# A planned order from one table of wanted times, in place of ranks, rounds and shifts

## The chip, the core and the metric

The kernel runs on one core of a Trainium2 chip. That core has TensorE (PE, with its weight loads as PEld), VectorE (DVE), ScalarE (ACT), GpSimd (POOL), and SyncE (SP), which here issues the transfers between HBM and the on-chip memories. The metric is the device time of one execution in microseconds. Three executions of the kernel before gave a median of 616.97 us (616.25 to 618.5). A difference of about 0.5% of that, some 3.1 us, is the smallest that a measurement of this kernel tells from no change.

## What is computed

The reference is one attention layer followed by one feed-forward layer, in float32:

```python
k_sum = k.reshape(B, H, nb, block, D).max(axis=3)
v_sum = v.reshape(B, H, nb, block, D).mean(axis=3)
scores_l = where(|i - j| < 16, scale * q @ k.T, -1e9)
scores_s = scale * q @ k_sum.T + log(block)
a = softmax(concat([scores_l, scores_s]))
attn = a @ concat([v, v_sum])
xn = (x - mean(x)) / sqrt(var(x) + 1e-6) * g_ln     # x = attn, heads side by side
out = x + relu(xn @ w_ch1) @ w_ch2
```

There are 4 batches, 8 heads, 768 positions, a head size of 64, blocks of 32 positions, a model width of 512 and a hidden width of 2048. So the attention is narrow (each row sees some 31 neighbours and 24 block summaries), and nearly all multiplications are those of the feed-forward layer.

## The kernel before

**Tiles.** The 3072 rows of x are 24 tiles of 128 rows. The first six tiles (batch 0, "early") are done with float32 products; the other eighteen ("late") with each operand split into two float16 halves. The names that the profile shows: `spare_x` holds the early keys, queries and values; `s` is a tile of scores; `p` the probabilities, `pp` their transposes, `o` the product with the values, `v` (on PE) the block means of the early values, `x` a finished tile of the attention, `xt` its normalised transpose. `raw` is a weight matrix as fetched, `m` the same with its bits merged by three DVE instructions (`merge_w`), `gram` small products that give its scale, `low` products that give the low half of a weight. `h` is the first product of the feed-forward layer (`g1`, L1005) and `a` the second (`g2`, L1028). A group of g1 takes two tiles of x, so there are twelve groups of eight steps.

**Order.** No engine's program is written in the order of the Python loops. `Plan` (L157 to L424) records every operation with its engine, its inputs and outputs; a list scheduler then decides the order, and `issue` (L402 to L424) emits the operations sorted by the start that the scheduler gave them. On each engine the chip runs them in just this order, so every record of the profile stands at one line, L425 of the profile's count. All of the transfers go through SP's one queue.

**The scheduler.** `schedule` (L341) walks through all 2808 operations. For each engine it keeps the operations that could start and takes the one with the lowest `rank`. It charges an operation its `busy` time from `cost` (L289); for a transfer it charges three numbers from the table `MOVE` (L175): the time on SP, the time that the transfer holds the queue, and the tail until its data may be read. It also holds TensorE's two clock levels, a cost for a change of kind on TensorE, and the port that DVE and POOL share. It runs forward or, with `back`, from the end to the start.

**Ranks before.** `issue` first gives each operation a rank by the longest way to the end, adds one number per stage from the table `ORDER`, runs `schedule` forward and backward up to three times (`ROUNDS`), keeps the best, adds one number per stage and engine from the table `SHIFT`, and runs forward once more. A stage is one call of a function that `@pl.step` marks, for example `early_qk(3)`.

The steps at the start that the prediction speaks of are these. `warm` (L1076) gives PE 36 transposes that need only `ident`. `gain` needs one small transfer, a PE product and some DVE instructions. `fetch_k0` brings the early keys in four transfers, `batch_k(0, hp)` reduces each on DVE to `kmax`, `early_k` (L800) puts the key tile together with copies on ACT and POOL, and `early_qk` (L810) is the product on PE. `fetch_v0` and `batch_v0` (L585, L592) bring six value tiles and a last piece, and add their block means in one chain of matmuls on PE. `clear` and `late_masks` are POOL's memsets and copies.

Of the kernel before, what the change touches and what calls it, by code (L numbers as in the profile page):

```python
# [24 lines left out]
B, H, S, D = 4, 8, 768, 64  # L25
# [18 lines left out]
ROUNDS = 3  # L44
# [11 lines left out]
    "c-k$Ne_YS^7RQfmchNQq`4MVX5)<o^a?>>{gl-`+tEP0f-7A}W$2FQq=K497MpWyngjs%cjYab-yRo#cmW^qqCE=<@`^81#b)P-"  # L56
    "De|#UG`h4E+_c`bFdY#vKXV*wcPnm7)V0L-"
    "4<dz|gIVxS+Cmkq|b{v$_&PmbFn$371<s6Z&d>}oP6wmkc15)u@W=+m!ryR`kk4uYcr3I{YoMqNI$!s<I@BK>}>S{J6*evy*(n0oSl=A+R6h>T"
    "^&Ss@gn}zev_c62ERnpFnCD%C4Zk8@^Zl`}pdpAgP*nj#8`?g5I?@0~;W)a=Yj;2b<Ig;@#x+@Lh%$GZwO(f?@=~DY|rKs<uz%gc3d!?_wmST5"
    "E$H;fuNOEP*iE62wnulDL#{b6bBfi}w##!<#`%p?fEnP2>dLEM||IKW7CiQxl?df86g0no&OaA2Cl{Jlh%%;9+Hjtd-"  # L60
    "Mw#{gRZ6LlvU-}02Djnl7sUUAe9Ue+nSDlnD~P|2wOJ>nL*#RY9M6?Yd5@S?4>Swrd3QKCk>AH|X70VsMzn{UpQQ))rRRAzuO-iEoC$uJJEf^N"
    "rD2DqDep@g{w+NjZZ>8QypmT2yyg*W*&Alv&PatHNeiDt3tOdH_Kiay1!Yp{CvZ*8yC8neHYtX8Q@}Bf8dChtZr*`&;@_dh>3<+LnwafqmOH@g"
    "L*9>yF<TO1=0wi*Xe=5|mY|~*5$t`^Yzw*=4fn+tSbI%sJuhdGSqzvY<x3INzVJ&a5v+YS!G))p%R1^oS6=8RA3hz)X-"
    "gBe@0M=B#SHY3g)U+~mo}lNkXup^Jbg?2fz-DKOuT=RuA&!*KcW@%8}PE(X0%fCgjxJXwD?;y=V#Duq**jN%YpwGwAX&M^cFpmPwbliN=v=X8b"
    "_P82gAX{^8({yu&IEr&Ob<RyokQ3FN>O1p|$N`eC;)}$9TVFzFEJnW{E@DKiKS<$I+}2e}P%p5Om|q9^xMZ!w}ZIfOZD7V*$0i&EMJe(sttYU1"
    "(NAkF_J;Pr*JBF5}3h?^*EpOnTPKYyyAxp+--"
    "%JDiwZs3CEJ*|KPKMID#G^)UKv2{hXuW;Pd0+<Sn@N@?a4vu_C7LOu!9dlG%TOJ2_r@5S+Ej`T`AdmHeN0q7(j?4scDI(_gH`aVO?A1Ia@&}$h"
    "QcR~BLW6kbgrB~2W&)=bCxClYJS?*?Oc+w<#-3JWLqQ779fxnacIzRfCc-`ST0{*KirB<IQ{*ivhcf!!zB`|-"
    "VXEfTrL4WxYs{~z)B$u)1=aE)i(be2X%`(vJ&v?!e>aEMBhxi^qzKxye|0pn~XWZfPYy<r9bVCQe<d%evX5a}<DR?6K@`8`jUS_e>9t_ql=w~O"
    "mJ&m6GliPzjsRQ^HvS)--8>YSSnkW~ul2(mv$3M_W5ghKu>&C*z=9y-TIj{Mm6b^R<=*|HwLdpG=-"  # L70
    "<u7Fi>Q8R6kg`h%l>F{7MMG6hAVyOk6uQDMJ_peqLuHSH=EV!+w|e%=;k6Z9wpWh-uGnRsz1Ro-qqCIY#JWF9&Kc@zi9=&OTTt+q-"
    "W^KfIp+NJbdxGv>KoHK|dS7`=wZB31^;0kMDu&LF#etZ*~RT%Zc;)A@U=Bf4prnG5&(DucWRQ*3kF#XCZ#(LLYDa1%Do9=1m``5GMhj-"
    "3wkhY0?+?Rwr;shO0&E;V?^@jYrQ!I}vc#fjn2SCVani3;!#?!|KrFc)o{n)<iTjFPGlHD_c0v6J8t0Gn8K4$R2OJsTXSlnMa@Cp_6wJ3s3bW#"
    "sPkd-<59Tg`umYCy4Eh52c`yJmUV9brs~ioxGfRABRRxv)+?^+jtkxFPu8MvNoNc2j6n>zb5idWUU*#=6x^S2cHq-"
    "Sb%Ql^V|vMo$!UdpQ2TG^8?3HX43H4W`5Kf!|y8k9z|d7p=aKqPuz;g58Ri6XAy>y8DzGN`Es8)<#_T@`tBxrPJpL7_?QQ}d<dp-oD;;^325de"
    "&T_!F3(-PX@-9N_3z!vE<P}M+6Tl&XXYE|GNa|^a2YwB9{W#Z;^-"
    "<)WON}0!yAfU8#BV;wUpMm%;`=#%=lQ+Kx{mnqJC~%xtc{>2Iug5ro@t=(yMbjY{ho_XGFP_gG4%h>`h9KB<9)enaK@L+Mt`*Khj-PX>q@k;8("
    "-M*74wGL50cMP@GK?YE@*Q(-yNr${Q&pwub90$6@O-bGhQ8ncE-`i>FD|)Ga?eb1TX`7fK_Y1MS@e0SLrG6F2U2wUZ-"
    "!E@4vuDGB|nSiAEeZJiiv4nkV5&XxXEM`stZ-@RG{?D;B=jl4BYDca44vWY&eil{?=T!c7`nw)X3Ba&Tl8rsH2ie?x-X=I<uFY9c-"
    "F!~G|cdOjf5d1`$CE_HbBKJZ)1-RCLvA?_$k=P)nUwQ2btYuA3kOa{+#=3)uwI?@9bVEH|s)Xe{<&@I;vJBiLu@V*I-"  # L80
    "FHmbTGoUWi%!_&}iG2gy+`f_C&Tiu*6})aUhc4suG4y*fx;18mE1De2y>K4f72pBO$)g=-bU<j+z-&D+@8M-"
    "N#EPRgqPYhRV@=w|HqRP|e%BML3eT-1u{r3j1g{&32ffCfg3)7n_(#@%z=&G2$?Xhxfh6jzC%?<|{(N-"
    "5pFEwJ0lmoMBD__TTQ#^G9l_nK^&W>VmXrIkLChlJ_CcRl@Z=xiyP6s1OMhKpE;=y73pwWmnpi!~Y&x~oaDFAcIN^_>c&i^Xw-"
    "Jug$)^R4xiYUam@k?1*CFO@5_i>DJbeKAIE*I*qN{pz(=ncYqqbvsSUSAaFbf{iZ%goCSMU!b?+M^hPF*$l*iblH%)MqZ|L<XsC-"
    "ZU_XZ{Z!wza_"
)
SHIFT = (
    "c-n<q34B%6(SO-NLV_TRtP(&Pftm`aZ3=z}h@?tE5<w!Os9;1=MA?LovI%aVh*1{V6cA9$5*9(x3W8CQAZ;ytAR?6=0z%j!$?Jde{+BoJzPWk%"
    "{Vw;ubLY%{X6DSf_<X^?(qH}liGII-R+-"
    "=LtKcvFMELuMFWGbE8@P(jhmSpKz|A$rc3%x2J5w4ycAvq^dSmQ0fB4*)QQ>gi4PJgS=8iPR#u#&J8E}&g{$>DfNsQ0eAJ4Iz)8<^@o@?l$hC%"  # L90
    "D;3*loQoeLdHG3Mo;4j)@lDV)c3m&4&YT?rq{y*_;IABqBSA651Cx3`r&cE$R92jc_J&&S&ESr`5O_AZ}z9sW63>0uE0D=Q9;#Q@*49z3Ka!3S"
    ";(Jm2a8Qw@A&oeib?d1arkYE1BVY~{fHUyAoM@OGQACSJw(ku!dOwg<frjWu`BfSYqN2-"
    "hgl=Nm;iUcb)9I}^IwToj6XHpbc{2Y>hG`(nlSKIo{qM;yq9-"
    "!!cic;0)}hWS10T;TGh4Cu5hDfoK;=awqEIaTcS9tB%$2EM;|#Ixcv;o}b(>$0ArHRp)m|8$MObIA!CZx!GucCD{lF!rF*cOK<@_h=BVE7m|Vb"
    "g<u8ukGPCqbWz_DBEsR5x-BlWIc+t5Tk6_hP)>!|I2}0YUBQ^3vVW_ZCEE0J?!<GF?PVv-x~GY8~pu)_<lTT<1L8x`8Gv|j{Smp$%>CLq|-"
# [70 lines left out]
class Plan:  # L166
# [174 lines left out]
    def schedule(self, rank, after, back):  # L341
# [16 lines left out]
        for _ in range(count):  # L358
# [27 lines left out]
            if e == "sync" and not back:  # L386
                t = max(t, flight[0])
# [855 lines left out]
```

## Time and profile before

| | us |
|---|---|
| median of three executions | 616.97 (616.25 to 618.5) |
| the profiled execution's own time | 614.86 |
| its span, from first to last instruction | 613.0 |
| PE busy in the span | 602.3 (98%) |
| DVE / ACT / POOL busy | 399.4 / 343.9 / 151.9 |
| mean granted TensorE clock | 0.997 |

In the rows, times are microseconds from the start of the span unless marked ns, `x16` is a count of instructions, and what stands in brackets with an arrow is how long the engine had been idle before the instruction and what ended that idle time. SPq and PEq are the engines' own sequencers. The profiled execution is 2.1 us shorter than the median of the three.

### The profile page before, as it was taken

The numbers are of one execution on the slowest core, as the hardware profiler recorded it, in microseconds if no ns is written. First come the engines' busy times: TensorE is split into PE (matmuls) and PEld (weight loads), VectorE is DVE, ScalarE is ACT, GpSimd is POOL, SyncE is SP. The second block draws the span as 40 slices with busy tenths as digits, with TensorE's granted clock in tenths as the row PEclk, the third lists the DMA queues.
The fourth block names the chain that finished last, engine by engine and source line by source line (L and its number), as shares of the span: only waits on it lengthen the run. The fifth ranks groups of instructions, "written<-read, shape, count | busy, mean of one in ns | idle before, by whom it ended". The sixth has DMA issues, their size and how long they took to land.

```text
span 613.0 us, 14238 instructions
## 1 busy us (share of the span) xinstructions
PE 602.3 (98%) x5347; PEld 414.0 (68%) x5347; DVE 399.4 (65%) x1098; ACT 343.9 (56%) x914; POOL 151.9 (25%) x279
## 2 busy tenths in 40 slices
PE   6999999999999999999999999999999999999997
PEld 5557778885454685676767864666775676678756
DVE  5799999998568379767694487367486574412211
ACT  3689986578867458576864364366465644111100
POOL 7232312102324124321331033133142333100000
PEclk9999999999999999999999999999999999999999
DMA  8989897454677636867886045526466332300000
GB/s 302 281 251 329 236 298 234 115 145 127 178 208 197 167 100 167 214 138 197 200 176 171 14 127 136 130 77 178 120 154 162 89 94 53 62 10 1 17 18 35
DMA packets 116396, 90.56 MB, mean 148 GB/s; under 512 B 69613, under 2 KB 100717, under 8 KB 116326
## 3 DMA queue, kind: packets, MB, share of 16 engines
q1 hardware_dynamic: 116326, 89.65, 54.1%
q8 instruction: 42, 0.69, 0.5%
q14 instruction: 28, 0.23, 0.1%
HBM read 67.05 MB, written 6.29 MB: 120 GB/s over the span
## 4 chain that ended last, share of the span: by engine, by line
PE 76%; DVE 10%; DMA 6%; ACT 4%; issue 2%; SPq 1%; POOL 1%; ACTq 0%; POOLq 0%
PE h L425 33%; PE a L425 31%; PE s L425 3%; DVE m L425 2%; PE o L425 2%; DMA bst<-in_ks 2%; PE low L425 2%; DMA bst<-in_qa 2%; SPq L425 1%; PE warm L425 1%; DVE kmax L425 1%; DMA qs<-in_qt 1%; DMA bst<-in_vs 1%; DVE h_x L425 1%; ACT p L425 1%
## 5 line engine op out<-in xcount | busy, mean ns | idle before, releaser
L425 PE MATMUL h<-xt,w_u 128*128 128x256 f16 x2304 | 264.1, 273 | 0.0
L425 PEld LDWEIGHTS <-w_u 128*128 128x128 f16 x2304 | 224.1, 98 | 37.1 <-issue 0.9
L425 PE MATMUL a<-w,h_x 128*128 128x512 f16 (+1 forms) x960 | 211.5, 374 | 0.1
L425 PEld LDWEIGHTS <-h_x 128*128 128x128 f16 x1008 | 97.8, 98 | 98.7 <-issue 0.4
L425 ACT ACTIVATE h_x<-h 128x512 f16<-128x512 f32 x80 | 46.8, 591 | 96.7 <-PE h L425 96.4
L425 DVE SCALAR_TENSOR_TENSOR h_x<-h,h_x 128x512 f16<-128x512 f32 x80 | 54.5, 684 | 68.1 <-ACT h_x L425 68.0
L425 ACT ACTIVATE p<-p,mn,sv 128x120 f32<-128x120 f32 x144 | 68.2, 475 | 10.0 <-POOL mn L425 9.9
L425 POOL TENSOR_TENSOR p<-p,p 128x480 f16<-128x480 f32 x36 | 42.5, 1184 | 64.1 <-ACT p L425 59.8
L425 ACT ACTIVATE bst<-bst 128x384 f32<-128x384 f32 (+2 forms) x55 | 32.3, 588 | 33.0 <-DVE vsum L425 12.7
L425 POOL TENSOR_SCALAR mn<-mn,sv 128x4 f32<-128x4 f32 x36 | 17.7, 491 | 114.4 <-DVE mn L425 110.4
L425 PE MATMUL a<-w,h_y 128*128 128x512 f16 x192 | 43.9, 379 | 0.0
L425 DVE SCALAR_TENSOR_TENSOR m<-raw,m 128x512 uint32<-128x512 uint32 x64 | 42.9, 681 | 0.2
L425 DVE SCALAR_TENSOR_TENSOR kl<-ksg,sv,kh 128x640 f16<-128x640 f32 x36 | 33.3, 925 | 11.6 <-ACT kh L425 11.3
L425 DVE CUSTOM_DVE_ANT_0 p<-s,mask 128x120 f32<-128x120 f32 x144 | 33.2, 274 | 11.1 <-PE s L425 9.1
L425 POOL TENSOR_TENSOR x<-x,rc 128x256 f32<-128x256 f32 x36 | 25.2, 706 | 52.1 <-DVE x L425 50.0
L425 DVE SCALAR_TENSOR_TENSOR qhl<-qs,sv,qhl 64x512 f16<-64x512 f32 x36 | 28.1, 779 | 12.2 <-ACT qhl L425 11.3
L425 ACT ACTIVATE v<-vst,sv 128x512 f16<-128x512 f32 x36 | 24.4, 712 | 19.6 <-PE o L425 17.8
L425 DVE SCALAR_TENSOR_TENSOR x<-a,scales,x 128x512 f32<-128x512 f32 (+1 forms) x24 | 17.7, 736 | 26.7 <-PE a L425 26.6
L425 ACT ACTIVATE kh<-ksg,sv 128x640 f16<-128x640 f32 x36 | 29.5, 819 | 9.3 <-DMA ksg<-in_kt 6.9
L425 ACT ACTIVATE qhl<-qs,sv 128x512 f16<-128x512 f32 x36 | 25.7, 713 | 13.6 <-DMA qs<-in_qt 10.2
L425 PEld LDWEIGHTS <-h_y 128*128 128x128 f16 x192 | 18.6, 98 | 20.2
L425 DVE SCALAR_TENSOR_TENSOR v<-vst,sv,v 128x512 f16<-128x512 f32 x36 | 27.2, 772 | 2.0 <-ACT v L425 1.9
(118 smaller groups left out, 698.8 us busy)
## 6 DMA issues: line engine op xcount, KB each, us to landing
raw<-in_w SPq DMA_DIRECT2D x32, 512.0 KB
ksg<-in_kt SPq DMA_DIRECT2D x36, 368.0 KB
qs<-in_qt SPq DMA_DIRECT2D x72, 128.0 KB
out_x<-x SPq DMA_DIRECT2D x23, 256.0 KB
bst<-in_ks SPq DMA_DIRECT2D x20, 192.0 KB
bst<-in_qa SPq DMA_DIRECT2D x15, 256.0 KB
bst<-in_vs SPq DMA_DIRECT2D x20, 192.0 KB
vst<-in_va SPq DMA_DIRECT2D x36, 96.0 KB
```

What stands on the lines that cost most here:

```text
L425: getattr(getattr(nc, self.ops[i].engine), op)(*a, **k)
```

## The change

The two tables `ORDER` and `SHIFT` and the constant `ROUNDS` go. A new `ORDER` holds one number for each of the 2808 operations: their running sum, times 16, is that operation's wanted time in ns, and the wanted time is its rank. `schedule` runs forward once; its backward form is deleted. Seven entries of `MOVE` get other numbers. What is computed, the operations, their tiles and buffers stay as they are; only the order in which each engine gets them can differ.

```diff
-        "T": (1320.0, 1370.0, 890.0),
+        "T": (1320.0, 1200.0, 1000.0),
...
-        (128, 2048): (420.0, 760.0, 1140.0),
-        (128, 2944): (460.0, 1660.0, 870.0),
-        (128, 3072): (450.0, 1390.0, 1420.0),
-        (128, 4096): (430.0, 1830.0, 1220.0),
+        (128, 2048): (420.0, 700.0, 1160.0),
+        (128, 2944): (460.0, 1350.0, 1000.0),
+        (128, 3072): (450.0, 1000.0, 1350.0),
+        (128, 4096): (430.0, 1500.0, 1400.0),
...
-    def schedule(self, rank, after, back):
+    def schedule(self, rank, after):
...
-                ring = max(ring, t if back else t + self.BEGIN) + moving
-                if back:
-                    free[e] = max(free[e], ring)
-                end[i] = ring + (self.BEGIN if back else 0)
+                ring = end[i] = max(ring, t + self.BEGIN) + moving
...
     def issue(self, nc):
-        after = [self.waits(x) for x in self.ops]
...
-        self.start, self.end = self.schedule(rank, after, False)
+        wanted = np.cumsum(np.frombuffer(zlib.decompress(base64.b85decode(ORDER)), "<i4"))
+        self.start, self.end = self.schedule(16.0 * wanted, [self.waits(x) for x in self.ops])
```

A key of `MOVE` is the number of partitions and the bytes in each; "T" is a transpose by DMA. So (128, 4096) is a 512 KB weight tile, (128, 3072) the 384 KB of an early key transfer, (128, 2944) the 368 KB of `ksg`, and (128, 2048) a 256 KB tile.

Unpacked from the diff and sorted by wanted time alone, without the scheduler, the table differs from the order before at nearly every place: 484 of PE's 516 operations, 885 of DVE's 906, 642 of ACT's 654, 269 of POOL's 273 and 439 of SP's 459 stand elsewhere, half of them by more than 7, 16, 18, 8 and 9 places. The wanted times are no starts: many are negative, and an operation whose inputs come late can carry an early one. It is then taken as soon as it is ready. Of what can start at once, SP's order begins before with key 1, gain, weight 1, query 0, keys 0, 3 and 2, weight 0, query 1, values 1, 2, 0, `blk`; by wanted time with gain, key 1, weight 1, query 0, keys 0, 3 and 2, value 2, weight 0, values 4 and 0, query 1, `blk`, values 1 and 3. Of the chain of seven `batch_v0` matmul steps on PE, the first has an earlier wanted time than any of the first four `early_qk` steps, the second a later one than any of them, and the other five early ones again (but each waits for the one ahead of it in the chain). Of what POOL can start with, the masks and `late_masks` come first, and the memsets of `clear` are wanted last.

## Rows read from the trace of the kernel before

**Rows 1.** The page: busy time of each engine with its share of the span, and the TensorE clock in 40 slices.

```profile
PE 602.3 (98%) x5347; PEld 414.0 (68%) x5347; DVE 399.4 (65%) x1098; ACT 343.9 (56%) x914; POOL 151.9 (25%) x279
...
PEclk9999999999999999999999999999999999999999
```

**Rows 2.** Busy time by stretch: the stretch, then its length, then busy us of PE, PEld, DVE, ACT and POOL with their instruction counts, the granted clock, the DMA engines' busy share and GB/s.

```profile
0.00:8.50 8.50, 6.64 (x37) 6.47 (x37) 2.77 (x4) 1.50 (x3) 7.55 (x31) 1.00 0.77 239
8.50:14.00 5.50, 2.01 (x20) 0.83 (x20) 4.32 (x13) 2.62 (x10) 3.70 (x22) 0.99 1.06 381
14.00:16.00 2.00, 1.98 (x20) 1.45 (x21) 1.97 (x9) 1.78 (x9) 0.68 (x3) 0.50 1.09 383
16.00:18.00 2.00, 2.00 (x28) 1.72 (x26) 1.05 (x10) 1.36 (x6) 0.53 (x3) 0.67 1.09 388
18.00:20.00 2.00, 2.00 (x13) 0.80 (x6) 1.50 (x11) 2.00 (x11) 0.70 (x4) 1.00 1.09 369
20.00:40.00 20.00, 18.27 (x168) 9.95 (x167) 17.65 (x63) 15.42 (x50) 5.50 (x16) 1.00 0.87 258
40.00:150.00 110.00, 109.89 (x1071) 84.24 (x1071) 104.62 (x287) 87.50 (x247) 22.99 (x48) 1.00 0.73 213
150.00:200.00 50.00, 49.89 (x371) 24.29 (x369) 33.04 (x99) 35.90 (x100) 16.60 (x22) 1.00 0.71 191
200.00:600.00 400.00, 400.00 (x3553) 275.99 (x3551) 230.79 (x604) 195.86 (x489) 93.65 (x134) 1.00 0.46 114
600.00:613.00 13.00, 9.65 (x87) 8.23 (x84) 1.72 (x3) 0.00 (x0) 0.00 (x0) 1.00 0.12 42
```

**Rows 3.** All waits of PE: who waited for whom, us in total, times, the longest.

```profile
PE s L425 <- DVE mn L425: 1.9, 1, 1.9
PE warm L425 <- POOL ident masks.py:199: 1.9, 1, 1.9
PE s L425 <- POOL spare_x L425: 1.6, 1, 1.6
PE s L425 <- ACT pT L425: 0.7, 1, 0.7
PE pp L425 <- DVE m L425: 0.4, 1, 0.4
PE low L425 <- ACT w_u L425: 0.3, 1, 0.3
PE pp L425 <- ACT p L425: 0.2, 1, 0.2
```

**Rows 4.** PE in order of time at the start: start, duration, operation; in brackets the idle time before it and its end.

```profile
1.86 6.67 PE L425 MATMUL warm<-ident 128*128 128x128 f32 x36 [1.86 <-POOL ident masks.py:199]
...
9.51 0.33 PE L425 MATMUL s<-ident 128*128 128x128 f32 x1
11.49 0.67 PE L425 MATMUL s<-spare_x,spare_x 64*64 64x128 f32 x16 [1.65 <-POOL spare_x L425]
14.02 0.44 PE L425 MATMUL s<-ident 128*128 128x128 f32 x1 [1.86 <-DVE mn L425]
...
17.25 0.30 PE L425 MATMUL s<-ident 128*128 128x128 f32 x1
...
18.08 1.98 PE L425 MATMUL v<-spare_x,blk 128*120 128x512 f32 x4
...
22.33 2.74 PE L425 MATMUL v<-spare_x,blk 128*120 128x512 f32 x6
...
44.80 1.47 PE L425 MATMUL h<-xt,w_u 128*128 128x256 f16 x12
```

**Rows 5.** DVE, then POOL, in order of time around the first product of scores.

```profile
9.62 0.69 DVE L425 TENSOR_REDUCE scales<-gain 128x1 f32<-128x512 f32 x1 [2.08 <-PE gain L425]
10.22 0.94 DVE L425 TENSOR_REDUCE kmax<-spare_x 128x24 f32<-128x768 f32 x1
...
11.34 0.94 DVE L425 TENSOR_REDUCE kmax<-spare_x 128x24 f32<-128x768 f32 x1
...
12.50 0.29 DVE L425 CUSTOM_DVE_ANT_0 p<-s,spare_x 128x128 f32<-128x128 f32 x1
...
12.72 0.95 DVE L425 TENSOR_REDUCE kmax<-spare_x 128x24 f32<-128x768 f32 x1
13.58 0.28 DVE L425 CUSTOM_DVE_ANT_0 p<-s,spare_x 128x128 f32<-128x128 f32 x1
```

**Rows 6.** The instructions on the tile spare_x up to 45 us: duration in ns as minimum/median/maximum, first and last start.

```profile
L425 POOL COPY spare_x<-spare_x x18: 230/236/779, 10.1 to 44.2; 128x64 f32<-128x64 f32 x18
L425 POOL COPY spare_x<-kmax x18: 197/202/764, 10.3 to 44.4; 128x24 f32<-128x24 f32 x18
```

**Rows 7.** The instructions on the tile raw, in the same form.

```profile
L425 DVE SCALAR_TENSOR_TENSOR m<-raw,m x64: 653/682/721, 6.1 to 116.4; 128x512 uint32<-128x512 uint32 x64
```

**Rows 8.** The chain that ended last, in order of time: two long pieces of the feed-forward stage (start, duration).

```profile
373.05 15.65 PE a L425 x72
388.69 7.86 PE h L425 x72
```

**Rows 9.** The last 13 us of the timeline, PE and DVE.

```profile
605.55 4.09 PE L425 MATMUL a<-w,h_x 128*128 128x256 f16 x36
...
609.69 0.48 DVE L425 SCALAR_TENSOR_TENSOR x<-a,scales,x 128x256 f32<-128x256 f32 x1 [3.45 <-PE a L425]
```

More of the change, by code (lines that the diff above doesn't have):

```diff
@@ L43 @@
 EH = 4
-ROUNDS = 3
 WARMQ = 4
@@ L55 @@
 ORDER = (
[L56 to L83, printed above, removed]
@@ new lines @@
+    "c-"
+    "k$R1$>uP7ssFVMmLNc(ltuyl#m$RF%gv)loV7_Is_#r4HD8IAuZkAjBd#R12zU@^}OF7=fBVH=RWt|)3?q!_kStDbu$DxPFR5Blz8mA7knLOt?"
+    "Rmu=WhyQHIrTU9dJ$3InJH8t~-nI*7P;@cAPP39H;CX*By}GaU$bfcYKKBd=1V4=<Sbn-Cooq6J56{v=aOsr*ypQzV~vR0moc-"
+    "9yAa8InF8QU4qs{;AZ(a&I`Uf15=5T4S5>9bKSGx=TC9nK8#(1_iW$>iDtCx)}S33=s4AYKmXo!y;D0*!z9-"
+    "|2JFbRj??V5>%N3fB=8@A%>}>EjE=MDh3giA=1%0=1aCgwN2wg=Ii(SeUFcc?n&r{!SwY8{iJm!QTz4cq)&Uy@+yQjV4ehkZGYVNlz`4p;AY+N"
+    "(<_Gsb>@ktPL$8nt*}ehhPIkx1o8EEu06dqv26T!8GZA~P1%5W)GviFA&CqQEtzO8u6rJwUj>L9pfm@FL!C4$<DKx(XW()}L(7hV41-"
@@ new lines @@
+    "x_*YX{UyFe`6=(NdUU0pD-xz4I%}>ap{j{I;l?ym8Y?cNdg~4scKKdKjQ^++5JzAsRQ@#hkvpC`m_=DlM8=Q;GVQP2|hj)MA=JWkM`*i|)z7zD"
+    "@z-PQ-8gwWJ{i5jH6+Fd}L!q%P-"
+    "t_yH{i=PQ8<;}$Plrzw`>q}E9hi$4CT9Y+3?w%Fi#ce)nNyte`6TvOmJ45&zRSc6!Qd=_PEX{h417#p&Q|6wC$jX1R}6eoST~BV>fR=f!%lUv("
+    "HUe&WGsp^qAYgrm4}!d`t#)vftv)6%HZ6`KJs14v(BCcDaeK|G6&K=i(dOUOTr7_`(e|~*if;305moN^9;Q6v<pDL33iWQeZ^zTS<onqys5!a{"
+    "Mi6LInXx(Jmm$FDBbCsgN*~Q#cuHPVWR}b&&zL>-"
+    "$t!?NU`4v>h<(3rf(_VTKCb=KLG81eBY#R4YC}9MrL@9K+dt)=??aYVtg$9_2}OSempW(V$C$gMwz&)Lv_xuCYfHR7;}`3^^t-"
@@ new lines @@
+    "O95qgRWD8(@_hX%80QWj_{{WxsjJ06CQv(;QH3N?#^jD;ByT{jTsQ5@e0Cvg-"
+    "kKW+u3=0EpD{$d7-YVv$o+tZI`zdY$CogqX#zs;XqaK3nWso5rdqq<}RGdgz0M01r4UugeiwB-kXGN}y*r&SaLnALT{6PJSVhs8F;OL%;r``@u"
+    "1>~8-"
+    "*lgMkcpn&>LI1yw$s`}xM==`fBNH}ifn8D<Q+#+A_^t94p&Npp<AB#bSOTq;J{I?Bz5fV}uRK2aRrF}fw_;MqbN?`9?k?aTQigo6Jdfs}0QlbE"
+    "7NNfe@Jr}tTHU_%Wu?T40R0OX&p|)S+SwwzFgA-i41UY$ucNa7f2cQiY$*45+54{BNInkxZv+0u=fJMQ&hvC0vF2VwFD-qWlWpE(lI@;t2hI-"
+    "m+gujRNcPh@bkD;+JIVRC3p;uvdytp;T;-@6(Y^@(l8kj^lSaau|BrSoq5C1g=AkTg2!-"
@@ new lines @@
+    "WDp#u5IDNGF|F@HEO>5u0LdNEd>-Pov4Nwu!np4brOmP^nb2M-Cl>}x7<+5^%)UCm<g6*d0E>|vAK8x-"
+    "MVC6S>`<fsAKGD|P2Jn`;mcLx2d8Ssra|tp$LeEUlJ1M_QZ_n%-<-"
+    "XI>zXX^NKU>GLt74sX@VbYddtX{EtR(&NaplkHeBCBq@?l)dS1Q+j3mQG>m*en6@s?vbSiSva@x-UY_}-"
+    "`YGUzGBl<wu>TNnI(iI%5Oe&zza4>7NkfLrKew(5?o%84A&J*GR1{vG-"
+    "~Bf6AMGQUpox%_(F*IM&_wEMZ{3)c6wxzhRchu$FcentC^=l6!cDW~LZdEBXtm*RT{{W@1_W2-"
+    "^L6VLTKNZk)f_S*pc9&!|PMk&{eJpJ?*;&1V}V!OZfHh^6gds`k{d7gKk{NE1cwSp`MqF8CQ^4}i+dm;Y8LEuNgU%#n2=6M$!$%PgeYq<^mCPK"
@@ L155 @@
+    "fJR32_WbiUT_(D+Wp*pJD!_jl=iF2UXhcIY>fdMAsu_s0uy7JuqDpt|=;QO~9Rnxfyt%thx!_-^D3-"
+    "1EWiE4{OY;yV<fzZ~C+x3l?KeAivSvte#y9lMM4TOK7XmA9H2Yww17PgfjT3g<-"
+    "cV*2fr?!7YL*G9ge)Ryztd9R#IK4|oWuJ)4NC6eRKS3Iu#UXtYnly^Iw)^g{2J^8ft-sb0Z;QOZZL&j3b5bJ9>K=})~MOS$}Z1F7C&X+Fslg5v"
+    "0YoedsW7?Pc?Wf+9^p+&rOOR7*KSD8{-jH33B?jtF*ZZ>eCjEMA)O>WbpP9JBz-"
+    ">gkvnOuSdXfJzRBwQR7Pl^<9Y*_%@}2VWboN0nMKL3M1C{T`F5mjt+jCoL(fvQN(kp5"
 )
@@ L351, in schedule @@
         coming, waiting = ({e: [] for e in self.ENGINES} for _ in range(2))
-        ring, warm, columns, tick = 0.0 if back else self.FIRST, False, 0.0, 0.0
+        ring, warm, columns, tick = self.FIRST, False, 0.0, 0.0
         port, half = 0.0, 0
@@ L356, in schedule @@
             if not left[i]:
-                heapq.heappush(coming[self.ops[i].engine], (0.0 if back else 1000.0, i))
+                heapq.heappush(coming[self.ops[i].engine], (1000.0, i))
         for _ in range(count):
@@ L375, in schedule @@
                 half = self.ops[i].half
-            if e == "tensor" and not back:
+            if e == "tensor":
                 while t >= tick + self.TICK:
@@ L385, in schedule @@
                 columns += (t + busy - at) * per
-            if e == "sync" and not back:
+            if e == "sync":
                 t = max(t, flight[0])
@@ L402, in issue @@
     def issue(self, nc):
-        after = [self.waits(x) for x in self.ops]
-        then = [[] for _ in after]
-        for i, x in enumerate(after):
-            for j, wait in x:
-                then[j].append((i, wait))
-        rank = [0.0] * len(after)
-        for i in reversed(range(len(after))):
-            x = self.ops[i]
-            rank[i] = min((rank[j] for j, _ in then[i]), default=0.0) - x.busy - x.moving - (self.WAIT[x.engine] or x.tail)
-        table = lambda x: 16.0 * np.frombuffer(zlib.decompress(base64.b85decode(x)), "<i4")
-        early, shift = table(ORDER), table(SHIFT).reshape(-1, len(self.ENGINES))
-        rank, best = [r + early[x.stage] for r, x in zip(rank, self.ops)], None
-        for _ in range(ROUNDS):
-            start, end = self.schedule(rank, after, False)
-            if best is None or max(end) < best[0]:
-                best = (max(end), start, end)
-            rank = [-x for x in self.schedule([-x for x in end], then, True)[1]]
-        rank = [r + shift[x.stage, self.ENGINES.index(x.engine)] for r, x in zip(best[1], self.ops)]
-        self.start, self.end = self.schedule(rank, after, False)
+        wanted = np.cumsum(np.frombuffer(zlib.decompress(base64.b85decode(ORDER)), "<i4"))
+        self.start, self.end = self.schedule(16.0 * wanted, [self.waits(x) for x in self.ops])
         self.time = max(self.end)
-        for _, i in sorted(zip(self.start, range(len(after)))):
+        for _, i in sorted(zip(self.start, range(len(self.ops)))):
             for op, a, k in self.ops[i].calls:
```

136 lines of the change are left out of this document (65 added, 71 removed).

## The prediction

> **What bounds the kernel now.** I read the page first, then the busy time by stretch, then PE's own waits, and last the timeline of the first 45 us. On the page PE is busy for 602.3 of 613.0 us, and its clock digit is 9 in every slice [rows 1]. So the time is PE's queue of work, and the question for a change of order is how much of the other 10.7 us an order can reach. The stretches answer it [rows 2]: from 40 to 150 us PE is busy for 109.89 of 110, from 150 to 200 for 49.89 of 50, from 200 to 600 for all of it. Nothing can be gained there by putting work into holes, because there are none. Nor do the matmuls themselves go below their pace there: in the chain 72 `h` matmuls take 7.86 us (109 ns each) and 72 `a` matmuls 15.65 us (217 ns each) [rows 8], so the 2304 and 1104 of full width take about 251.5 and 239.9 us wherever they stand.
>
> The list of PE's waits says the same [rows 3]: seven waits, together 7.0 us, and by the timeline the two long ones are at 9.8 to 11.49 us and at 12.2 to 14.02 us [rows 4]. The 1.86 us ahead of `warm` is the wait for `ident`, which is made outside of the plan; no table moves it. At the other end the last matmul ends at 609.6 us (605.55 + 4.09), and after it come 0.48 us of DVE and the last store, 3.4 us up to the end of the span [rows 9]; the plan cannot shorten that pair. So the waits that the change can reach are 1.65 + 1.86 at the front and 0.7 + 0.4 + 0.3 + 0.2 = 1.6 us behind them: 5.1 us.
>
> There is a second loss at the same place. After these two waits the granted clock is 0.50 from 14 to 16 us and 0.67 from 16 to 18 us, with PE busy for all but 0.02 us of it [rows 2]. At the lower level, 1.2 GHz, the 2.0 us and the 0.66 us (x at half and 2 - x at full, mean 0.67, gives x = 1.32, so 1.32 us at half) are 3.3 us in which PE got at most half of what it does at 2.4 GHz: up to 1.65 us.
>
> **The change part by part.** Nothing is added to or taken from the chip's work: the instructions are the same, so a term of the sum can only be a wait that goes, comes or changes place.
>
> 1. *The second hole, 12.2 to 14.02 us.* PE stands at the warm transpose of the second `s` because its two buffers wait for DVE, which does two `kmax` reductions of 0.94 and 0.95 us among the score instructions [rows 5]. There is other work for PE that depends on none of this: the chain of `v` matmuls, which now runs from 18.08 us (1.98 us for four) and from 22.33 us (2.74 us for six) [rows 4]. By the table, three value transfers (2, 4, 0) now go ahead of query 1, and the first `v` step is wanted early, so it is taken as soon as its data are there. From above the hole is filled whole, 1.86 us; from below not at all, if the values land after it. One of the chain's seven steps is two matmuls, about 1 us (1.98 us for four), so it takes two of them with their transfers to fill the hole; I take 1.4 us, nearer to the upper end. The cost of the move: query 1 stands behind three more transfers of 256 KB, at the 381 GB/s of that stretch [rows 2] 0.69 us each, together 2.1 us; its cover is that its product (`s` of the third head group) starts only at 17.25 us [rows 4].
>
> 2. *The first hole, 9.8 to 11.49 us.* It ends when POOL has put `kmax` into the key tile, and that `kmax` starts on DVE at 10.22 us, behind the reduction of `gain` (9.62 us, 0.69 us), which itself had DVE idle for 2.08 us ahead of it [rows 5]. If the reduction of the key goes first, the product starts up to 0.6 us earlier; if also the transfer lands earlier, up to 1.2 us. From below 0, and below nothing if DVE is sent to a weight's merge at that point (its instructions are 0.68 us each [rows 7]): -0.7 us. In the table `gain` is still wanted just ahead of that `kmax`, so I take little, 0.5 us.
>
> 3. *The four small waits, 1.6 us.* Each is one operation too early on PE with other work behind it. From 0 to 1.6 us; a rank per operation in place of one per stage can part two operations of a stage that went together before. I take half, 0.8 us.
>
> 4. *The clock.* It fell after a stretch in which PE was busy for 2.01 of 5.5 us [rows 2]; nowhere after 18 us, with PE busy for nine tenths and more, does it fall again. From 0 to 1.65 us; with the two holes about half as long I take 1.0 us.
>
> 5. *New waits.* After 40 us there are none now worth naming (0.11 + 0.11 us of PE's idle time up to 200 us [rows 2]). With 885 of DVE's 906 places changed some will come. From 0 to the price of the slower rival below; I take 0.3 us, one small wait of today's size [rows 3].
>
> 6. *The transfer table.* The plan's numbers change nothing on the chip by themselves, but they decide how tight the order is cut. In 14 to 18 us the queue is full (share 1.09) and moves 383 to 388 GB/s [rows 2]. At 385 GB/s a 256 KB transfer is 0.68 us, one of 384 KB 1.02 us, one of 512 KB 1.36 us. The old table said 0.76, 1.39 and 1.83 us, the new one 0.70, 1.00 and 1.50. So at the front the new numbers are nearer, and transfers land as the plan says or a little earlier. From 20 to 40 us the rate is 258 GB/s at a share of 0.87 [rows 2], where 512 KB would take 2.0 us; that bounds it on the other side, 0.5 us late for each weight. I take nothing here, since a weight goes to DVE's merge first and not to PE.
>    The Trainium skill, page DMA: Bandwidth & Descriptors, section Where 436 GB/s comes from, gives some 358 GB/s as the limit of one core's share of HBM, which would make 384 KB take 1.10 us and each key transfer land 0.1 us later than the new table has it. The trace does not agree: 381 to 388 GB/s over 10 us [rows 2]. By the page the sum would lose 0.3 us for three keys; the measured rate decides, and it loses nothing.
>
> The sum: 1.4 + 0.5 + 0.8 + 1.0 - 0.3 = 3.4 us. Against the profiled execution's 614.86 us that is 611.5 us; the median of the runs shown is 2.1 us above that execution, so the forecast for the median is 616.97 - 3.4 = 613.6 us. With every term at its upper end, 1.86 + 1.2 + 1.6 + 1.65, it would be 6.3 us, 610.7 us.
>
> **The rivals.**
> *The holes only move (no change).* Both front holes hang on chains: key transfer, reduction, copy, product, score instruction. DVE is busy for 4.32 of the 5.5 us from 8.5 to 14 us [rows 2]. If what fills PE's hole is missing later, when the chain has still not delivered (20 to 40 us, PE 18.27 of 20 [rows 2]), the sum of the holes stays 5.1 us. For it: nearly two microseconds of hole are still there at 20 to 40 us although PE has had `v`, `gram` and `low` to choose from. Against it: from 40 us on PE is never short, so work done earlier is never missed. Time 616.9 us.
>
> *DVE starves PE between 40 and 150 us (slower).* There DVE is busy for 104.62 of 110 us [rows 2]: 5.4 us free. It merges the weights, three instructions each, and evicts the `h` tiles that PE must have back. The new order shuffles just this engine most. If at some places a merge (0.68 + 0.68 + 0.4 us, about 1.8 us [rows 7]) comes ahead of an eviction that PE needs, PE waits for it; today that never happens. At six places it costs 6 x 1.8 = 10.8 us, at four 7.2. Less the 3.4 us of the front, four to five places give some 4.5 us more than before: 621.5 us. It decides from about 3.4 + 3.1 = 6.5 us of waits on PE after 40 us. For it: DVE's full share. Against it: the scheduler is greedy and never leaves PE idle in its own account, and today's order, made by the same account with slower transfers, left 0.22 us.
>
> *POOL's copies are blocked by DVE (small gain).* POOL's copies into the key tile take 236 ns, but at worst 779 ns, and those of `kmax` 202 and 764 [rows 6]; 764 - 202 = 0.56 us is near one DVE merge instruction of 0.68 us [rows 7]. If the merges come forward into the first products, four copies on the way to the first four products are held for 0.55 us each: 2.2 us. 616.97 - 3.4 + 2.2 = 615.8 us. The Trainium skill, page SBUF — State Buffer, section Who interferes with whom, says that a DVE instruction with two inputs in SBUF and a GpSimd instruction that reads SBUF exclude each other for the whole instruction; the merge has two such inputs, so the page and the maximum in the row point the same way, and by the page each copy that meets a merge pays.
>
> *The front is filled whole.* All terms at their upper ends, 610.5 us.
>
> **How the numbers follow.** Forecast, gains of 1 to 5.5 us: 0.60. No change: 0.10. Slower: 0.18. Blocked copies: 0.05. Filled whole: 0.07. About 0.5%, 3.1 us, can be told from no change, so faster is below 613.9 us. Of the forecast's 0.60 some 0.36 lie there, with 0.07 from the whole filling: 0.43. Within 0.5%: 0.24 + 0.10 + 0.05, less 0.02 that the bounds leave on the slow side: 0.37. Slower: 0.20. The range that leaves out 2 in 10 goes from 610.3 us to 620.3 us, which is to the middle of the slower rival. The likeliest case alone has 611.5 to 616 us.
>
> **What would show it.** Right: the list of PE's waits is shorter by the `s` wait on DVE `mn`, `v` matmuls stand between 12 and 16 us, the clock from 14 to 18 us is well above 0.6, and PE is still busy for all but 0.3 us from 40 to 150 us. Wrong: waits of PE for `h` tiles or weights after 40 us, a first `s` product later than 12 us, or the same 5 us of holes at other places. Step 6 is wrong if the trace has 20 to 40 us with DVE waiting for `raw` for more than a microsecond.

## The result, and the profile after

The kernel after takes 622.65 us in the median of 15 executions (618.16 to 625.21); the kernel before, on the same chip, 616.56 us (15 executions). One of the kernel after's took 3548.5 us and is left out of the range and the ratio, as one of 620.71 us of e10 below is left out of e10's ratio; that one is the profiled execution, so no row of e10 is read. The ratio is 1.0083 with an interval of 1.006 to 1.0105: slower by about 6 us, where 613.6 us was forecast and 620.3 us was the upper end of the range. The profiled execution took 621.93 us; its span is 620.1 us against 613.0 before.

On the page of after, PE's busy time and the clock answer to [rows 1]. PE is busy 2.7 us longer and idle 4.4 us longer (15.1 us in place of 10.7), and one slice has a clock digit of 8:

```profile
PE 605.0 (98%) x5347; PEld 415.0 (67%) x5347; DVE 400.8 (65%) x1098; ACT 345.4 (56%) x914; POOL 146.7 (24%) x279
...
PEclk9989999999999999999999999999999999999999
```

Busy time by stretch, in the columns of [rows 2], says where:

```profile
8.50:14.00 5.50, 3.01 (x41) 1.63 (x39) 4.74 (x19) 2.41 (x11) 2.41 (x15) 1.00 1.05 369
14.00:16.00 2.00, 1.62 (x21) 1.03 (x14) 2.00 (x11) 1.80 (x9) 1.51 (x4) 0.70 1.09 385
16.00:18.00 2.00, 2.00 (x8) 0.50 (x7) 1.95 (x8) 1.77 (x9) 0.00 (x0) 0.50 1.09 387
...
20.00:40.00 20.00, 18.15 (x162) 10.48 (x161) 16.96 (x59) 14.81 (x47) 3.94 (x13) 0.91 0.90 269
40.00:150.00 110.00, 106.34 (x1047) 82.19 (x1046) 99.48 (x273) 85.06 (x237) 20.50 (x46) 1.00 0.72 203
150.00:200.00 50.00, 49.06 (x368) 24.00 (x367) 31.67 (x98) 35.94 (x99) 15.14 (x25) 1.00 0.75 183
200.00:600.00 400.00, 399.38 (x3549) 275.53 (x3547) 237.18 (x620) 200.53 (x501) 94.83 (x136) 1.00 0.47 116
```

Of the 4.4 us of idle time that PE has more, 3.55 us lie between 40 and 150 us (3.66 us idle in place of 0.11), 0.83 between 150 and 200 us, and 0.62 behind that; the front up to 20 us is 0.64 us better. The granted clock explains most of the 2.7 us of busy time: from 20 to 40 us it is 0.91 where it was 1.00 (all of it between 30 and 40 us), which is 3.6 us at the lower level, 1.2 GHz, and so 1.8 us of work lost. DVE moves the other way from PE: from 40 to 150 us it does 5.1 us less (99.48 us, against 104.62). It is not too busy for PE; both fall behind together.

PE's waits, the first seven of ten rows, against the seven of [rows 3]:

```profile
PE s L399 <- DVE scales L399: 2.5, 1, 2.5
PE warm L399 <- POOL ident masks.py:199: 1.9, 1, 1.9
PE h L399 <- DVE h_x L399: 1.4, 2, 1.1
PE o L399 <- ACT p L399: 1.3, 1, 1.3
PE a L399 <- DVE x L399: 1.2, 2, 0.9
PE h L399 <- DMA xt<-x: 1.2, 2, 0.8
PE low L399 <- ACT w_u L399: 1.0, 1, 1.0
```

No single wait is large, and their releasers are four different things. To see whether they have one origin, two of PE's waits were followed back on the releasing engine. The timelines show first PE's wait for ACT and what ACT did ahead of it, then what DVE did ahead of PE's other wait, and that wait:

```profile
83.54 0.70 PE L399 MATMUL low<-m,diag 128*128 128x512 f32 x1 [0.99 <-ACT w_u L399]
```
```profile
75.30 0.63 ACT L399 ACTIVATE bst<-bst 128x512 f32<-128x512 f32 x1 [1.04 <-DMA bst<-in_qa]
...
76.94 0.63 ACT L399 ACTIVATE qs<-qs 128x512 f32<-128x512 f32 x1 [0.92 <-DMA qs<-in_qa]
```
```profile
115.08 0.68 DVE L399 TENSOR_REDUCE vsum<-bst 96x16 f32<-96x512 f32 x1 [1.58 <-DMA bst<-in_vs]
115.68 1.38 DVE L399 SCALAR_TENSOR_TENSOR m<-raw,m 128x512 uint32<-128x512 uint32 x2
117.08 0.69 DVE L399 SCALAR_TENSOR_TENSOR h_x<-h,h_x 128x512 f16<-128x512 f32 x1
```
```profile
117.82 1.36 PE L399 MATMUL h<-xt,w_u 128*128 128x256 f16 x11 [1.15 <-DVE h_x L399]
```

At 76.94 us ACT has stood idle for 1.04 and 0.92 us, because the next instruction of its program reads a query tile of batch 1 that has not landed; the copies into `w_u` stand behind it in the same program, and at 83.54 us PE waits 0.99 us for one. At 115.08 us DVE has stood 1.58 us for a value tile; two merges and the eviction of `h` stand behind it, and PE waits 1.15 us for that eviction. In both places a small statistics step (`batch_q` L595, `batch_v` L583) stands at the place where its transfer should have landed, and blocks the work behind it that PE needs. The chain of after from 66 to 120 us goes through the same transfers, with four legs of 4 to 6 us from issue to landing; that of the kernel before has two there, of 3.26 us at 104.94 us and 3.71 us at 119.26 us, and a short one of 1.26 us:

```profile
71.43 5.42 DMA qs<-in_qa
...
83.54 1.34 PE low L399 x3
...
87.64 6.12 DMA raw<-in_w
93.79 0.43 DVE m L399
...
100.37 4.26 DMA qs<-in_vs
104.66 0.60 DVE vsum L399
...
111.23 3.83 DMA bst<-in_vs
```

A third wait has a transfer itself as its end. `xt`, the tile of x that PE multiplies, comes out of a DMA transpose in the same queue; the transpose's entry "T" is one of the seven that changed. In the kernel before, the first two transposes are issued from 38.52 us, with no weight issued in the 7 us ahead of them, and have landed at 42.97 us. The new order issues two weights and a key tile of batch 1 just ahead of them (37.67 to 38.85 us), they land at 46.29 us, and the first `h` waits for them. In e2 and e7, two kernels of the next section that begin in the new order with whole transfers, this is the longest wait of PE from 40 to 125 us; the kernel before, e1, e5 and e6 have none. The first line is after's, the others are those of e2 and e7:

```profile
46.34 0.83 PE L399 MATMUL h<-xt,w_u 128*128 128x256 f16 x6 [0.81 <-DMA xt<-x]
```
```profile
PE h L340 <- DMA xt<-x: 3.1, 1, 3.1
```
```profile
PE h L341 <- DMA xt<-x: 2.2, 1, 2.2
```

Whether the delay also feeds itself, by merges that free a weight's buffer late and so hold back the next fetch, isn't shown: from 20 to 125 us SP waits 17.7 us for `DVE m`, where before it was 11.8, but all of its listed waits come to 59.6 us against 58.4.

How far the queue strays from the table can be read from the landings in the two traces. Of the transfers that were issued at least 3 us before the one ahead of them landed, so that the queue had work, the 512 KB weights landed 1.35 us (median) and 1.46 us (mean) behind that one before, over 19 weights, and 1.39 and 1.59 us after, over 18; single ones took up to 2.03 and 2.73 us. (With all weights that were issued before the one ahead landed, 32 and 31, the medians are 1.65 and 1.84 us.) The 256 KB tiles of `batch_q` have 0.72 and 0.91 us before, over 8, and 0.68 and 0.86 us after, over 6, in the whole run; in the first 130 us, where the loss lies, their means are 0.72 and 0.64 us, over 5 and 3. So the new table's 1.50 and 0.70 are near the middle of what the queue does, and leave little for the single late ones. The old table's 1.83 for weights was above both median and mean.

### The profile page after: what moved, and what is told of

Same layout as the page of the kernel before. It is cut to its first block, busy times and chain, and to the rows that moved or that the text cites. A ratio compares the mean times of both kernels' runs of the same rounds, so it can differ in the third digit from the quotient of the medians.

```text
span 620.1 us, 14220 instructions
## 1 busy us (share of the span) xinstructions
PE 605.0 (98%) x5347; PEld 415.0 (67%) x5347; DVE 400.8 (65%) x1098; ACT 345.4 (56%) x914; POOL 146.7 (24%) x279
## 4 chain that ended last, share of the span: by engine, by line
PE 78%; DMA 9%; DVE 6%; ACT 4%; issue 1%; SPq 1%; POOL 0%; ACTq 0%; POOLq 0%
PE a L399 34%; PE h L399 33%; PE s L399 3%; PE o L399 3%; DVE m L399 2%; DMA qs<-in_qa 2%; DMA bst<-in_vs 2%; PE warm L399 1%; DMA qs<-in_ks 1%; PE low L399 1%; DMA raw<-in_w 1%; DMA bst<-in_qa 1%; PE last L399 1%; SPq L399 1%; DMA bst<-in_ks 1%
## 5 line engine op out<-in xcount | busy, mean ns | idle before, releaser
L399 DVE SCALAR_TENSOR_TENSOR h_x<-h,h_x 128x512 f16<-128x512 f32 x80 | 53.9, 684 | 58.4 <-ACT h_x L399 58.0
L399 DVE SCALAR_TENSOR_TENSOR x<-a,scales,x 128x512 f32<-128x512 f32 (+1 forms) x24 | 17.7, 736 | 40.8 <-PE a L399 40.7
L399 POOL TENSOR_SCALAR mn<-mn,sv 128x4 f32<-128x4 f32 x36 | 15.4, 428 | 92.6 <-DVE mn L399 87.7
L399 DVE TENSOR_REDUCE x<-o 128x256 f32<-128x512 f32 x36 | 23.7, 683 | 10.8 <-PE o L399 10.7
```

What stands on the lines that cost most here:

```text
L399: getattr(getattr(nc, self.ops[i].engine), op)(*a, **k)
```

## The experiments

Theory T: the order is cut to transfer times that the queue does not hold, and the loss arises in the first 125 us or so, where 24 MB of weights and batch 1's inputs go through the queue. Rivals: the loss is spread over the whole order (S), the new transfer numbers by themselves do the harm (T1), a table of wanted times fits only the numbers for which it was made (F), and the engines' own work is in a worse order whatever the transfers do (D).

**The first 125 us alone.** Two kernels have their order written out; `issue` only reads it, and `ORDER` holds the place of each operation. The first has the order before up to 125 us and the order after behind it, the second the reverse.

```diff
-        for _, i in sorted(zip(self.start, range(len(self.ops)))):
+        place = np.cumsum(np.frombuffer(zlib.decompress(base64.b85decode(ORDER)), "<i2"))
+        for i in np.argsort(place):
```

> The two orders are written out, nothing is planned: every operation that the order before started in its first 125 us keeps that order's place, the rest follow in the order of the changed kernel. Theory T: the loss arises between 20 and 115 us, where the new order needs transfers earlier than the queue delivers them, and behind that stage PE is full in either order. Then this runs like the kernel before: 616 to 617.5 us, and PE waits less than 0.6 us in all between 40 and 200 us. Rival S, the loss is spread over the whole run because nearly every place has changed: half of it stays, 619 to 620 us.

> The mirror image: the first 125 us in the order of the changed kernel, the rest in the order before. Theory T: the loss is all there, 621.5 to 623.5 us. Rival S: half of it, 619 to 620 us. T and S cannot both hold with e1 and e2 in the middle.

Measured: 616.12 us (615.08 to 618.27), ratio 0.9996 (0.9979 to 1.0012), and 622.39 us (619.25 to 623.22), ratio 1.0087 (1.0066 to 1.0107). The stretch from 40 to 125 us of the first and of the second:

```profile
40.00:125.00 85.00, 84.26 (x857) 65.41 (x856) 79.31 (x226) 66.22 (x201) 19.80 (x38) 1.00 0.80 235
```
```profile
40.00:125.00 85.00, 79.96 (x775) 60.65 (x772) 73.10 (x209) 61.89 (x190) 17.52 (x40) 0.96 0.78 224
```

The whole loss goes with the first 125 us; S falls. What after's order does behind 125 us costs nothing by itself. One detail of the expectation missed: in the first kernel PE is idle for 1.10 us from 40 to 200 us, not for less than 0.6.

**Table and numbers apart.** After with the old seven entries of `MOVE`, and before with the new ones:

```diff
-        (128, 4096): (430.0, 1500.0, 1400.0),
+        (128, 4096): (430.0, 1830.0, 1220.0),
...
```
```diff
-        (128, 4096): (430.0, 1830.0, 1220.0),
+        (128, 4096): (430.0, 1500.0, 1400.0),
...
```

> One part of the change undone: the table of wanted times stays, the seven transfer entries go back to the slower numbers. Theory T1, the faster numbers alone do the harm because with them the planner counts on data too early: with the slower ones it orders more safely and the time falls to 616 to 620 us. Rival F, a table of wanted times fits only the account it was made with, and under another one the same numbers give an arbitrary order: 630 us or more, with waits of PE by far longer than 2.5 us.

> The other part of the change alone: the kernel before with its ranks, rounds and shifts, and only the seven transfer entries changed. T1: the planner now cuts too tight and the time goes to about that of the changed kernel, 619 to 624 us. Rival F: the old tables were made for the old numbers as well, and the order falls apart: 630 us or more.

Measured: 637.78 us, ratio 1.0344 (1.032 to 1.0368), and 655.38 us, ratio 1.0629 (1.0605 to 1.0654). Either half alone is far worse than both together: some 21 and 39 us. Of the second, much of the loss lies at the start: PE is idle for 6 us from 20 to 40 us (1.7 before) and for 15 us from 40 to 125 us, at a clock of 0.84 and 0.88; another 9 us of idle time lie from 200 to 600 us. In the first no wait of PE is far longer than 2.5 us, as F had it: the longest has 2.8.

```profile
20.00:40.00 20.00, 13.93 (x168) 9.39 (x167) 17.10 (x65) 13.81 (x54) 4.63 (x18) 0.84 1.05 305
40.00:125.00 85.00, 69.94 (x611) 47.07 (x612) 73.24 (x223) 63.80 (x198) 21.98 (x45) 0.88 0.77 220
```

So F holds: ranks and numbers belong together, and the seven numbers reach the chip only through the order that they make. This also means that the pair cannot show which numbers are better. T1 in its plain form falls, since the old numbers under the new table lose still more.

**Fewer bytes at the same order.** Both orders written out, and the 22 statistics transfers of batch 1 cut to half their bytes. The halved tile is read twice on DVE, so DVE's work stays; ACT's sum of absolute values runs over half. All three kernels so leave half of batch 1 out of its statistics. The third is the control: after's order, that half ACT work, and full transfers.

```diff
-                nc.sync.dma_start(kk, ks[b, hp, :, cs])
+                part = ks[b, hp, :, cs]
+                if b == 1:
+                    kk, part = kk[:, :6], part[:, :6]
+                nc.sync.dma_start(kk, part)
...
-        nc.sync.dma_start(x[:], qa[b, :, c * DM : c * DM + DM])
+        k = n
+        nc.sync.dma_start(x[:, :k], qa[b, :, c * DM : c * DM + k])
```

> The changed kernel's order written out, with one thing less: the 22 transfers that bring batch 1 for its statistics between 20 and 116 us carry half their bytes (some 2.2 MB less, about 6 us of the queue at its rate of that stretch); DVE reads each half twice, so its work stays, and ACT's 22 Abs instructions shrink to half. Half of batch 1 is so left out of the block means, block maxima and scales. Theory T: PE was late because these and the transfers behind them landed late, so most of the loss goes: 617 to 619.5 us. Rival D, it is the order of the engines' own work (merges ahead of evictions) that keeps PE waiting: 621.5 to 623 us, as the changed kernel.

> The same halved transfers and Abs instructions under the order before, written out. Theory T: that order does not wait for them, so nothing moves: 615.5 to 617.5 us. If fewer bytes help any order, by rival D or because all engines run lighter, it gains as much as the run above.

> The control for the first run of this call: the changed kernel's order with the transfers whole again, but ACT's 22 Abs instructions still over half of each tile. Theory T: the shorter Abs instructions give little, 621 to 623 us. If they were what helped, this is as fast as the run with halved transfers.

Measured: 618.04 us (615.48 to 621.25), ratio 1.0036 (1.0015 to 1.0057); 615.14 us, ratio 0.999 (0.9974 to 1.0005); 622.32 us, ratio 1.0105 (1.0085 to 1.0124). In the same order (the first and the third, e5 and e7) the 2.35 MB less are worth 4.3 us of the 6.5 that the control is behind the kernel before; in the order before (e6) they are worth nothing that can be told (0.4 us below the time expected). From 40 to 125 us, the first and the third:

```profile
40.00:125.00 85.00, 83.45 (x843) 64.50 (x842) 78.49 (x227) 62.88 (x202) 18.83 (x42) 1.00 0.73 204
```
```profile
40.00:125.00 85.00, 80.33 (x793) 61.82 (x792) 74.34 (x217) 59.18 (x193) 17.97 (x41) 0.98 0.80 226
```

T holds against D for two thirds of the loss: nothing but bytes differs between these two, and PE gets 3.1 us back. The last third (618.04 against 615.82) stays with transfers that were not halved or with the engines' own order; this pair doesn't part them. Part of it lies ahead of 40 us: from 20 to 40 us the clock is 0.83 in e5, 0.91 in the control and 1.00 before. One reading is to be kept out: DVE's wait for `raw` from 20 to 125 us is longer in the faster kernel, 5.7 us, than in the control, 2.9 us. A sum of DVE's waits for one tile is no measure of the harm, since DVE may wait there with nothing behind it that PE needs.

```profile
DVE m L341 <- DMA raw<-in_w: 5.7, 7, 1.6
```
```profile
DVE m L341 <- DMA raw<-in_w: 2.9, 5, 1.3
```

**An order with a margin.** If an order fails because it counts on one set of transfer times, one that holds under later transfers too should keep its gain. Both kernels begin from the order before, and a random search moves single operations that start in the first 170 us, by up to 14 places in their own engine's program; what comes behind stays as it was. In the first kernel the search goes by the mean of the planner's end over three sets of transfer times: the new numbers, and 1.12 and 1.2 times them, each with another starting moment of the planner's clock account. In the second the new numbers decide alone. The edit is that of the first pair, with other contents of `ORDER`.

> A written-out order, found by trying exchanges that start from the order before and keeping what ends earlier under all of three sets of transfer times: the new numbers, and 1.12 and 1.2 times them. Nothing else differs from the kernel after. Theory (the change lost its time because its order counts on transfer times that the queue keeps only at the median): an order that also works with later transfers keeps its gain on the chip, 611 to 614.5 us, ratio 0.990 to 0.996, with 40 to 125 us at 84.5 us or more of PE. Rival (the margin doesn't matter, only how far the search went): the same time as e9_search_single within 1 us.

> The same search from the same start, but judged under the new transfer numbers alone, without any margin. Theory: slower than e8_search_bounds by 1 to 5 us, 614 to 619 us, and what it loses lies in waits for transfers or for DVE work behind transfers between 20 and 125 us. Rival (the margin doesn't matter): the same time as e8_search_bounds within 1 us.

Measured: 611.26 us (609.99 to 614.18), ratio 0.9933 (0.9909 to 0.9958), and 616.09 us (614.68 to 619.36), ratio 1.0006 (0.9991 to 1.0021). The first search also ran longer, in two stages; but under the new numbers alone the planner sees the two orders as equally long (606.4 and 606.5 us). To see whether one order had been lucky, both searches were done again with another seed:

> The search of e8_search_bounds with another seed, so another order with the same margin. If the margin made the gain: 610 to 613.5 us, ratio 0.989 to 0.996. If e8 was one lucky order: anywhere from 611 to 618 us, as likely beside e11_search_single_b as ahead of it.

> The search of e9_search_single with another seed: the new transfer numbers alone, no margin. If the margin decides: 614 to 619 us, at least 2 us behind e10_search_bounds_b. If it doesn't: within 1 us of it, or ahead.

Measured: 613.66 us (610.67 to 620.71), ratio 0.9942 (0.9916 to 0.9968), and 622.29 us (619.22 to 624.41), ratio 1.0096 (1.0064 to 1.0128). Both orders with a margin are faster than the kernel before, both without one are not, and the second of those is as slow as the change itself. The theory's own bounds were missed twice: e10 by 0.2 us above 613.5, and e11 by 3.3 us above 619. PE from 40 to 200 us, in the kernels before, after, e8, e9 and e11:

```profile
40.00:200.00 160.00, 159.78 (x1440) 108.52 (x1440) 137.66 (x385) 123.40 (x345) 39.59 (x69) 1.00 0.72 206
```
```profile
40.00:200.00 160.00, 155.40 (x1413) 106.19 (x1412) 131.15 (x370) 121.00 (x335) 35.64 (x71) 1.00 0.73 196
```
```profile
40.00:200.00 160.00, 159.77 (x1416) 108.92 (x1409) 138.16 (x384) 123.44 (x344) 42.31 (x76) 1.00 0.76 214
```
```profile
40.00:200.00 160.00, 156.04 (x1369) 105.65 (x1367) 133.76 (x374) 120.37 (x335) 37.96 (x72) 1.00 0.70 203
```
```profile
40.00:200.00 160.00, 154.30 (x1363) 104.14 (x1360) 132.75 (x370) 119.21 (x330) 33.01 (x73) 1.00 0.72 202
```

The two orders that hold (before, whose numbers were too slow for weights and so had a margin by accident, and e8) leave PE idle for 0.22 and 0.23 us there; the three that are cut to the new numbers alone (after, e9, e11) for 4.60, 3.96 and 5.70 us. (Of e9's, 2.42 us lie behind 125 us, later than its expectation had them.) What e8 gains over the kernel before lies ahead of that: its clock stays up from 14 to 20 us, where before and after have 0.72, and that is worth 1.7 us (0.28 x 6); PE is busy for 3.32 us in place of 2.01 from 8.5 to 14 us; and the transposes of `warm` end 1.15 us sooner in this execution.

```profile
14.00:20.00 6.00, 5.99 (x50) 3.08 (x49) 4.94 (x26) 4.55 (x19) 1.91 (x8) 1.00 1.09 380
```

The clock's part is no luck of one execution: the mean clock is 0.999 to 1.000 in all six of e8 and 0.991 to 0.997 in those of the kernel before beside the searches. That the margin did it isn't shown, as the search had several starting moments of the clock as well. The margin is shown for 40 to 200 us.

The planner's own account says the same of all six orders. It can be run over an order as it is written out, with any transfer numbers; the columns give its end in us, an estimate, with the seven old numbers, with the new ones, and with the new ones where every transfer holds the queue 1.12 and 1.2 times as long:

| order | old numbers | new numbers | new, 1.12 | new, 1.2 | measured median |
|---|---|---|---|---|---|
| before | 613.7 | 613.2 | 613.3 | 616.3 | 616.56 |
| after | 620.1 | 611.7 | 617.7 | 627.8 | 622.65 |
| e8 (margin) | 611.1 | 606.4 | 609.0 | 612.0 | 611.26 |
| e10 (margin) | 610.5 | 606.2 | 608.9 | 612.7 | 613.66 |
| e9 (none) | 614.6 | 606.5 | 613.3 | 621.1 | 616.09 |
| e11 (none) | 616.8 | 606.2 | 615.2 | 622.1 | 622.29 |

Under the new numbers after is better than before by 1.5 us, and the four searched orders are alike. Under the old numbers after is worse by 6.4 us (measured 6.1), and both orders with a margin are ahead of both without, as on the chip. So as a judge of a finished order the old, slower numbers were the better ones here, though the new ones are nearer to the median landing.

## Why the prediction was wrong, by its own steps

- *What bounds the kernel.* Right for the kernel before, and read too far: since PE was idle for 0.22 us from 40 to 200 us, this stretch could only lose, and the change to every engine's order put all of it at stake. The order before was full there because it had slack (the table above moves it by 0.1 us from 1.0 to 1.12), not because any order would be.
- *Step 1, the second hole (1.4 us taken).* Wrong: it grew from 1.86 to 2.49 us. The first `v` step did come forward, but only to 15.81 us, behind the hole. Nor could the second have filled the rest with it, as the step had it: the table wants that one later than any of the first score products. The hole's cause stayed as well: DVE again takes two `kmax` ahead of the first score instruction, as in [rows 5].

```profile
10.67 0.94 DVE L399 TENSOR_REDUCE kmax<-spare_x 128x24 f32<-128x768 f32 x1
...
11.59 0.94 DVE L399 TENSOR_REDUCE kmax<-spare_x 128x24 f32<-128x768 f32 x1
...
12.51 0.28 DVE L399 CUSTOM_DVE_ANT_0 p<-s,spare_x 128x128 f32<-128x128 f32 x1
```

- *Step 2, the first hole (0.5 us taken).* Right in kind and too small: the first product of scores starts at 10.21 us without a wait, 1.28 us earlier than at [rows 4]; the upper bound was 1.2.

```profile
10.21 0.67 PE L399 MATMUL s<-spare_x,spare_x 64*64 64x128 f32 x16
...
13.37 0.30 PE L399 MATMUL s<-ident 128*128 128x128 f32 x1 [2.49 <-DVE scales L399]
```

- *Step 3, four small waits (0.8 us).* Three of them went; `low` still waits for `w_u`, 1.0 us in place of 0.3; and others of the same size came.
- *Step 4, the clock (1.0 us).* Wrong: with a hole of 2.49 us left, it fell as before, to 0.70 and 0.50 from 14 to 18 us, and once more between 30 and 40 us, which was not foreseen.

```profile
30.00:40.00 10.00, 9.35 (x96) 6.10 (x97) 8.85 (x33) 7.47 (x17) 2.54 (x5) 0.83 0.71 212
```

- *Step 5, new waits (0.3 us).* Badly mis-sized: behind 20 us PE is idle for 5.1 us more (0.12 from 20 to 40 us, then 3.55 + 0.83 + 0.62). The 885 of DVE's 906 places that the step speaks of were those of the table sorted alone; in the order that ran fewer differ, 755 of DVE's, 340 of PE's 516, 501 of ACT's 654, 136 of POOL's 273 and 327 of SP's 459, and half of each engine's operations moved by two places at most. A smaller change than it reckoned with cost more.
- *Step 6, the transfer table. This is the step that failed.* It saw that 512 KB could land half a microsecond later than the table has it, and took nothing for that, "since a weight goes to DVE's merge first and not to PE". In-order engines pass a delay on: what waits is not the merge alone but everything behind it in DVE's and ACT's programs, evictions and `w_u` copies among it, and these do go to PE. The step also looked at weights only; two of the waits followed above come from batch 1's query and value tiles, and the third, for `xt`, comes straight from the queue to PE. The price that it put at nothing: in the same order, 2.35 MB less in the queue give back 4.3 us of 6.5 (e5 against e7). Its witness (DVE waiting for `raw` from 20 to 40 us for more than a microsecond) was set on the wrong tile and stretch: it reads 0.5 us, and so says nothing of the loss.
   The trace of after bears out the measured rate on which the step decided: 387 GB/s from 16 to 18 us, not the 358 GB/s that the Trainium skill gives, page DMA: Bandwidth & Descriptors, section Where 436 GB/s comes from. The mean rate was right; single landings were not at the mean. The row of the witness:

```profile
DVE m L399 <- DMA raw<-in_w: 0.5, 2, 0.3
```

- *The rival "DVE starves PE between 40 and 150 us"* gave 621.5 us and had the stretch right, with a chance of 0.18; its sign, waits of PE for `h` tiles after 40 us, came (1.4 us). That its time is near is in part luck: it took some 8 us of new waits less 3.4 us won at the front, and there were 5.0 us after 40 us, 0.64 us won at the front and 1.8 us lost to the clock. Its mechanism is half there: at 115.68 us two merges do stand ahead of the eviction that PE needs. But DVE had stood idle for 1.58 us before them and is less busy there than in the kernel before. It was short of data, not of time. What was put against this rival, that the scheduler never leaves PE idle in its own account, is the very trap: the account and the chip differ by the landings.
- *"The holes only move", and "filled whole".* Neither: the front as a whole won 0.64 us. (The second is given as 610.7 and as 610.5 us; its sum gives 610.7.) *Blocked POOL copies:* PE has no wait on POOL's copies in after, so the rule of the Trainium skill, page SBUF — State Buffer, section Who interferes with whom, decided nothing here.

## What to carry to other kernels

An order written out against one set of durations is only as good as its slack where it meets the memory system. In an in-order engine one small step that is planned for the very moment at which its data should land holds up all that stands behind it, so judge an order under several sets of transfer times before keeping it, and keep the tables and the numbers they were made with together. When the bounding engine is full only because everything else comes in time, a change of order there can lose and not win: price its rival first, and look for waits on any transfer, on every engine that feeds the full one.

## What was not expected of the hardware

- In a queue with work, 512 KB transfers land behind the one ahead of them at a steady median (1.35 us before, 1.39 us after) with wide strays: 1.21 to 2.03 us before, 0.98 to 2.73 us after.
- Executions of one fixed order spread over several us: 618.16 to 625.21 us after, 613.71 to 618.5 us before, 609.99 to 614.18 us for e8, 614.68 to 619.36 us for e9. e10, with a margin, went from 610.67 to 620.71 us, so a margin makes an order faster here but isn't shown to make it steadier.
- PE's first transposes run at 213 ns from start to start and later at 109 ns, while the column of the granted clock says 1.00 for both. The change comes at 7.0 us in the kernel before and 4.8 us in e8, where the 36 take 6.67 and 5.52 us. The order doesn't decide when: in after, e2, e5 and e7, with one order at the start, it comes at 7.9, 5.3, 4.9 and 7.5 us. No run settles why. The stretch from 4 to 6 us in the kernel before and in e8:

```profile
4.00:6.00 2.00, 2.00 (x12) 2.00 (x11) 1.29 (x2) 0.00 (x0) 1.81 (x8) 1.00 1.05 257
```
```profile
4.00:6.00 2.00, 2.00 (x16) 2.00 (x16) 1.05 (x2) 0.52 (x2) 1.81 (x9) 1.00 0.90 284
```
